# Two layers' weight tiles moved to other byte offsets within their SBUF partitions

## The chip, the core and the metric

The kernel runs on one core of a Trainium2 chip. The metric is the device time of one execution in microseconds (us). The median of three runs of the kernel before is 1143.83 us (1143.75 to 1143.92). The trace shown here is of one further execution, which took 1143.75 us; between its first and its last instruction lie 1142.0 us, called its span.

## The reference, cut to what matters

x has the shape (2, 4096, 192), all in float32. A causal convolution with seven taps per head comes first, then two feed-forward layers on 8192 tokens, each with its own w_in (192 x 2048) and w_out (2048 x 192):

```python
w = softmax(weight)                      # (8 heads, 7 taps)
x = conv(x, w)                           # per head of 24 channels, causal
h = x @ w_in1;  g = h * clip(h + 3, 0, 6) / 6;      x = g @ w_out1
h = x @ w_in2;  g = where(h > 0, h, exp(min(h, 0)) - 1);  out = g @ w_out2
```

## The kernel before, in words

Everything is kept transposed: channels on the partitions, tokens along the free dimension. The 8192 tokens are worked in 16 blocks of 512 tokens, 256 of either batch. A layer's 2048 hidden units are cut in 16 slices of 128, so a "slot" is one layer, one block, one slice; there are 2 x 16 x 16 = 512 slots, in an order written out by hand in `slots`.

To keep float32 accuracy with the type fp32r, each operand is split in a high and a low part. For a slot, `mm1` (L490 in the trace) issues five matmuls into a PSUM bank `h`: the high weights `wi{l}h` with the token operands opA and opB, the low weights `wi{l}l` with opA, and `wi{l}r` (the channels past 128, high in one half of the partitions and low in the other) with opC and opD. VectorE and ScalarE turn `h` into `g` and split it into `gh` and `gl`. Four slots later `mm2` (L533) issues five matmuls per slot with the second weights `wo{l}`: three with gh, two with gl.

From the 36th slot on each matmul is cut into a lower half (partitions 0 to 63) and an upper half (64 to 127), which the array runs side by side; two generators, `lower` and `upper`, hand them to TensorE's queue in turn, one of each. Each matmul instruction brings its own weight load (LDWEIGHTS, shown as engine PEld): 64 or 128 rows by 128 columns of four bytes, which is 512 bytes of each partition, or by 66 columns. The next weights are loaded while the current matmul streams its 512 tokens.

The weights stay in SBUF for the whole kernel, in the pool `const`, which has one buffer for each name. In a partition wi0h, wi0l, wi0r, wi1h, wi1l and wi1r take 8192 bytes each, wo0 and wo1 24,576 each. They are written only once: `load_w` brings raw 64-bit numbers in by DMA, `decode` makes float32 of them, and `split_w` writes the parts by a ScalarE copy and one or two VectorE subtractions. This goes on beside the matmuls until about 292 us; in the first 31 us the matmuls wait for it and for the convolution.

Places in SBUF: the program puts 16 KiB of descriptors and a few constants ahead of the pools, so that `const` begins at byte 16,512 of each partition, which is 32 x 512 + 128. The unused tile `gap0` (96 words, 384 bytes) moves wi0h to byte 16,896 = 33 x 512. All weight tiles are multiples of 512 bytes long, so each of them, and each of their 128-column pieces, begins at a multiple of 512. The tokens' operands (opA to opD, gh, gl) begin at multiples of 512 as well. Not all tiles do: `heads`, a stationary operand of the first matmuls, begins 160 bytes past one, and the convolution reads `xT0` and `xT1` from 320, 384, 448 and 480 bytes past one, and from one to six words further on for the later taps.

The lines that the change touches are these; the rest of the kernel refers to the tiles through `wi[l]` and `wo[l]` only:

```python
const.tile([P, 96], F32, name="gap0")
cv.tile([P, 80], F32, name="gap1")
wi = [{n: const.tile([P, FF], F32R, name=f"wi{l}{n}") for n in ("h", "l", "r")} for l in range(2)]
wo = [const.tile([P, NF, 2 * D], F32R, name=f"wo{l}") for l in range(2)]
```

Of the kernel before, what the change touches and what calls it, by code (L numbers as in the profile page):

```python
# [8 lines left out]
F32 = mybir.dt.float32  # L9
F32R = mybir.dt.float32r  # L10
# [7 lines left out]
P = 128  # L18
# [37 lines left out]
def conv_moe_moe2(ctx: ExitStack, tc: tile.TileContext, x, weight, w_in1, w_out1, w_in2, w_out2, out):  # L56
# [18 lines left out]
    B, S, D = x.shape  # L75
    H, K = weight.shape
    FF = w_in1.shape[1]
    NT = B * S
    NF = FF // P
# [10 lines left out]
    const = ctx.enter_context(tc.tile_pool(name="const", bufs=1))  # L90
# [10 lines left out]

    w_in = (w_in1, w_in2)
    w_out = (w_out1, w_out2)
    const.tile([P, 96], F32, name="gap0")
    cv.tile([P, 80], F32, name="gap1")
    wi = [{n: const.tile([P, FF], F32R, name=f"wi{l}{n}") for n in ("h", "l", "r")} for l in range(2)]
    wo = [const.tile([P, NF, 2 * D], F32R, name=f"wo{l}") for l in range(2)]

    ident = few.tile([P, P], F32, name="ident")
    relay = few.tile([1, 1], F32, name="relay")  # L110
# [192 lines left out]
    def conv_r(b):  # L303
        a = yield from taps_vector(b, 1)
        lh, hl = opnd[0, b][2:]
        T0, T1 = slice(0, HB), slice(HB, NB)
        act.copy(hl[LO, T0], a[LO])
        act.copy(lh[UP, T1], a[UP])
        yield
        act.copy(lh[UP, T0], a[LO])  # L310
        act.copy(hl[LO, T1], a[UP])
        yield
        vec.tensor_tensor(out=lh[LO, T0], in0=a[LO], in1=hl[LO, T0].bitcast(F32), op=ALU.subtract)
        vec.tensor_tensor(out=hl[UP, T1], in0=a[UP], in1=lh[UP, T1].bitcast(F32), op=ALU.subtract)
        yield
        act.copy(hl[UP, T0], lh[LO, T0].bitcast(F32))
        act.copy(lh[LO, T1], hl[UP, T1].bitcast(F32))
        yield
# [366 lines left out]
    with tc.manual_schedule():  # L685
# [13 lines left out]
        r = conv_r(0)  # L699
# [97 lines left out]
    with tc.manual_schedule():  # L797
        ends = {}
        n = {LO: 0, UP: BEHIND}
# [47 lines left out]
```

## Time and profile before

| | |
|---|---|
| median of three runs | 1143.83 us (1143.75 to 1143.92) |
| profiled execution | 1143.75 us |
| its span | 1142.0 us |
| PE (matmul) busy | 1132.0 us, 99%, 9507 instructions |
| PEld (weight load) busy | 1020.9 us, 89%, 9507 instructions |
| DVE (VectorE) busy | 918.7 us, 80% |
| ACT (ScalarE) busy | 929.7 us, 81% |
| granted TensorE clock, mean | 0.999 |

Busy means that at least one instruction of the engine was in flight. Matmuls are pipelined: one takes 386 ns from its start to its end, but the next of the same half starts long before that end, so the pace is read from starts. The weight loads overlap the matmuls.

### The profile page before, as it was taken

The page shows a single profiled execution, that of the slowest core. Times are in us where ns is not written, and L with a number is a line of the kernel's source. Part 1 is how long each engine was busy: PE and PEld are TensorE (multiplying, and loading weights), DVE is VectorE, ACT ScalarE, POOL GpSimd, SP SyncE. Part 2 cuts the span into 40 slices and gives each one's busy share as a digit, 9 for nine tenths or more (in the row PEclk, how much of TensorE's full clock was granted, in tenths as well). Part 3 has the DMA queues.
Part 4 walks back from the last instruction along what each step waited for, and adds up shares of the span by engine and source line. Part 5 has one row for each costly group of instructions (what it writes and reads, how often), then busy time and mean ns, then how long its engine had stood idle before and what let it go on. Part 6 is the DMA issues. An engine that isn't in the chain of part 4 may idle for free.

```text
span 1142.0 us, 25136 instructions
## 1 busy us (share of the span) xinstructions
PE 1132.0 (99%) x9507; PEld 1020.9 (89%) x9507; DVE 918.7 (80%) x1560; ACT 929.7 (81%) x1685; POOL 44.7 (4%) x490
## 2 busy tenths in 40 slices
PE   8999999999999999999999999999999999999998
PEld 6788998988888999999999999999988889888887
DVE  7997999988887968778687887968767666677765
ACT  6876777788888787887878878787886888898986
POOL 0000000000000000000000000000000000000000
PEclk9999999999999999999999999999999999999999
DMA  6422012010010100101001010100000000000001
GB/s 184 112 66 44 22 43 47 29 29 1 2 29 1 27 3 4 26 2 28 2 13 18 1 29 1 24 7 1 15 2 15 2 10 6 15 15 15 13 6 26
DMA packets 105370, 26.80 MB, mean 23 GB/s; under 512 B 96416, under 2 KB 104096, under 8 KB 105248
## 3 DMA queue, kind: packets, MB, share of 16 engines
q1 hardware_dynamic: 104960, 24.99, 10.3%
q8 instruction: 74, 1.21, 0.5%
q14 instruction: 48, 0.39, 0.1%
q10 hardware_dynamic: 288, 0.20, 0.1%
HBM read 18.87 MB, written 6.29 MB: 22 GB/s over the span
## 4 chain that ended last, share of the span: by engine, by line
PE 96%; DVE 2%; ACT 1%; issue 0%; ACTq 0%; DVEq 0%
PE p L533 50%; PE h L490 46%; ACT u L50 1%; DVE acc L50 0%; DVE xw L50 0%; ACT opC L50 0%; DVE g L50 0%; DVE gl L50 0%; ACT opD L50 0%; DVE wi0r L50 0%; DVE cw L50 0%; DVE diag L50 0%; ACT L50 0%; DVE wo L50 0%; ACT gh L50 0%
## 5 line engine op out<-in xcount | busy, mean ns | idle before, releaser
L533 PE MATMUL p<-gh,wo 64*128 64x512 f32 (+1 forms) x2978 | 598.5, 386 | 0.0
L50 DVE SCALAR_TENSOR_TENSOR g<-u,h 128x512 f32<-128x512 f32 x512 | 350.0, 684 | 190.3 <-ACT u L50 185.3
L533 PE MATMUL p<-gl,wo 64*128 64x512 f32 (+2 forms) x1985 | 481.5, 386 | 0.0
L533 PEld LDWEIGHTS p<-gh,wo 64*128 64x128 f32 (+1 forms) x2978 | 433.6, 184 | 28.9 <-ACT gh L50 0.2
L50 DVE TENSOR_TENSOR gl<-g,gh 128x512 fp32r<-128x512 f32 x512 | 350.2, 684 | 2.9 <-ACT gh L50 2.4
L50 ACT CAST gh<-g 128x512 fp32r<-128x512 f32 x512 | 311.3, 608 | 13.4 <-DVE g L50 13.1
L533 PEld LDWEIGHTS p<-gl,wo 64*128 64x128 f32 (+1 forms) x1985 | 292.0, 160 | 20.6 <-DVE gl L50 0.4
L50 ACT ACTIVATE u<-h,three 128x512 f32<-128x512 f32 x256 | 176.1, 688 | 103.6 <-PE h L490 101.1
L50 ACT ACTIVATE u<-h 128x512 f32<-128x512 f32 x256 | 152.6, 596 | 55.3 <-PE h L490 54.4
L490 PE MATMUL h<-opA,wi1h 64*128 64x512 f32 x512 | 182.6, 388 | 0.2
L490 PE MATMUL h<-opA,wi1l 64*128 64x512 f32 x512 | 182.2, 388 | 0.0
L490 PE MATMUL h<-opB,wi1h 64*128 64x512 f32 x512 | 181.5, 386 | 0.0
L490 PE MATMUL h<-opA,wi0h 64*128 64x512 f32 (+1 forms) x476 | 170.8, 389 | 0.5 <-ACT opA L50 0.3
L490 PE MATMUL h<-opB,wi0h 64*128 64x512 f32 (+1 forms) x476 | 170.4, 387 | 0.0
L490 PE MATMUL h<-opA,wi0l 64*128 64x512 f32 (+1 forms) x476 | 170.3, 387 | 0.0
L50 ACT ACTIVATE u<-u 128x512 f32<-128x512 f32 x256 | 161.9, 632 | 8.3
L490 PE MATMUL h<-opC,wi1r 64*128 64x512 f32 x384 | 140.5, 386 | 0.0
L490 PE MATMUL h<-opD,wi1r 64*128 64x512 f32 x384 | 140.4, 386 | 0.0
L490 PE MATMUL h<-opC,wi0r 64*128 64x512 f32 (+1 forms) x366 | 135.1, 387 | 0.6 <-ACT opC L50 0.6
L490 PE MATMUL h<-opD,wi0r 64*128 64x512 f32 (+1 forms) x366 | 134.9, 387 | 0.0
L50 DVE SCALAR_TENSOR_TENSOR acc<-xT,taps,acc 128x256 f32<-128x256 f32 (+1 forms) x180 | 105.6, 603 | 0.1
L490 PEld LDWEIGHTS h<-opA,wi1h 64*128 64x128 f32 x512 | 94.2, 184 | 7.9 <-DVE g L50 2.7
(89 smaller groups left out, 1213.3 us busy)
## 6 DMA issues: line engine op xcount, KB each, us to landing
raw<-in_moe_w_out_dram SPq DMA_DIRECT2D x16, 384.0 KB, 3.2
out_dram<-z SPq DMA_DIRECT2D x180, 32.0 KB, 1.6
raw<-in_moe_w_in_dram SPq DMA_DIRECT2D x7, 512.0 KB, 4.0
x_sq<-in_x_dram SPq DMA_DIRECT2D x112, 32.0 KB, 2.2
raw<-in_moe_w_in_dram SPq DMA_DIRECT2D x8, 256.0 KB, 3.9
xr_sq<-in_x_dram SPq DMA_DIRECT2D x56, 32.0 KB, 2.2
x_sb<-in_x_dram SPq DMA_DIRECT2D x4, 128.0 KB, 3.6
raw<-in_moe_w_in_dram SPq DMA_DIRECT2D x4, 128.0 KB, 3.5
```

The source lines that it names most:

```text
L50: return fn(*args, **kw)
L490: mm = nc.tensor.matmul(h, k, m[half], start=low and i == 0, stop=high and i == len(todo) - 1)
L533: nc.tensor.matmul(p[:n, cols], k[:, :n], m[half, cols], start=first and not end and k is not w0l, stop=last and end == 1 and cols.stop == NB)
```

## The change

The 384 bytes of `gap0` are dealt out in three parts: 128 bytes ahead of layer 1's weights, 192 between the layers, 64 behind. The order of the tiles becomes wi0h, wi0l, wi0r, wo0, wi1h, wi1l, wi1r, wo1. Layer 1's weights now begin at 16,640 = 32 x 512 + 256, layer 2's at 16,640 + 49,152 + 192 = 65,984 = 128 x 512 + 448. The pool ends at byte 115,200 as before, so that every other tile stays at its place. No instruction is added, removed or put in another order.

```diff
     w_in = (w_in1, w_in2)
     w_out = (w_out1, w_out2)
-    const.tile([P, 96], F32, name="gap0")
     cv.tile([P, 80], F32, name="gap1")
-    wi = [{n: const.tile([P, FF], F32R, name=f"wi{l}{n}") for n in ("h", "l", "r")} for l in range(2)]
-    wo = [const.tile([P, NF, 2 * D], F32R, name=f"wo{l}") for l in range(2)]
+    wi, wo = [], []
+    for l, ahead in enumerate((32, 48)):
+        const.tile([P, ahead], F32, name=f"gap{l + 2}")
+        wi.append({n: const.tile([P, FF], F32R, name=f"wi{l}{n}") for n in ("h", "l", "r")})
+        wo.append(const.tile([P, NF, 2 * D], F32R, name=f"wo{l}"))
+    const.tile([P, 16], F32, name="gap4")
```

## Rows read from the trace of the kernel before

**Rows 1.** The page's chain of work that ended last: by engine, by line.
```profile
PE 96%; DVE 2%; ACT 1%; issue 0%; ACTq 0%; DVEq 0%
PE p L533 50%; PE h L490 46%; ACT u L50 1%; DVE acc L50 0%; DVE xw L50 0%; ACT opC L50 0%; DVE g L50 0%; DVE gl L50 0%; ACT opD L50 0%; DVE wi0r L50 0%; DVE cw L50 0%; DVE diag L50 0%; ACT L50 0%; DVE wo L50 0%; ACT gh L50 0%
```

**Rows 2.** That chain in order of time, 500 to 520 us: start, duration (us), work.
```profile
503.86 0.91 PE p L533 x8
```

**Rows 3.** PE by form: rows*columns of weights, count | busy us, mean ns | idle.
```profile
L533 PE MATMUL p<-gh,wo 64*128 64x512 f32 x2878 | 570.7, 386 | 0.0
L533 PE MATMUL p<-gl,wo 64*128 64x512 f32 x1019 | 346.3, 386 | 0.0
L533 PE MATMUL p<-gl,wo 64*66 64x512 f32 x900 | 319.4, 386 | 0.0
L490 PE MATMUL h<-opA,wi1h 64*128 64x512 f32 x512 | 182.6, 388 | 0.2
...
L490 PE MATMUL h<-opA,wi0h 64*128 64x512 f32 x440 | 156.9, 388 | 0.0
...
L490 PE MATMUL h<-opC,wi1r 64*128 64x512 f32 x384 | 140.5, 386 | 0.0
...
L490 PE MATMUL h<-opC,wi0r 64*128 64x512 f32 x330 | 121.0, 386 | 0.0
...
L533 PE MATMUL p<-gh,wo 128*128 128x512 f32 x96 | 27.0, 389 | 0.0
...
L490 PE MATMUL h<-opA,wi0h 128*128 128x512 f32 x36 | 13.9, 396 | 0.5 <-ACT opA L50 0.3 <-DVE g L50 0.2
```

**Rows 4.** PEld, the weight loads, by form.
```profile
L533 PEld LDWEIGHTS p<-gh,wo 64*128 64x128 f32 x2882 | 415.6, 184 | 25.1 <-ACT gh L50 0.2 <-ACT y L50 0.2
...
L533 PEld LDWEIGHTS p<-gl,wo 64*66 64x66 f32 x900 | 119.5, 133 | 7.4
...
L533 PEld LDWEIGHTS p<-gh,wo 128*128 128x128 f32 x96 | 18.0, 188 | 3.8
```

**Rows 5.** Timeline, 704.3 to 705.2 us: start, duration (us), engine, line, work.
```profile
704.48 0.43 PE L533 MATMUL p<-gl,wo 64*66 64x512 f32 x2
704.57 0.18 PEld L490 LDWEIGHTS h<-opA,wi1h 64*128 64x128 f32 x1
...
704.71 0.39 PE L490 MATMUL h<-opA,wi1h 64*128 64x512 f32 x1
704.71 0.18 PEld L490 LDWEIGHTS h<-opB,wi1h 64*128 64x128 f32 x1
...
704.94 0.39 PE L490 MATMUL h<-opB,wi1h 64*128 64x512 f32 x1
```

**Rows 6.** Timeline, 566.5 to 567.2 us.
```profile
566.64 0.46 PE L533 MATMUL p<-gl,wo 64*66 64x512 f32 x2
566.75 0.18 PEld L490 LDWEIGHTS h<-opA,wi1h 64*128 64x128 f32 x1
...
566.87 0.39 PE L490 MATMUL h<-opA,wi1h 64*128 64x512 f32 x1
```

**Rows 7.** The convolution's second stretch of matmuls, timeline of PE.
```profile
17.40 6.21 PE L290 MATMUL psc<-xT,diag 128*128 128x256 f32 x28
```

**Rows 8.** Loads of the tile heads: duration min/median/max (ns), first and last start (us).
```profile
L211 PEld LDWEIGHTS pt<-etap,heads x4: 283/328/328, 3.9 to 4.5; 8*128 8x128 f32 x4
```

**Rows 9.** Loads of the tile diag, in the same view.
```profile
L290 PEld LDWEIGHTS psc<-xT,diag x56: 187/189/337, 6.6 to 23.0; 128*128 128x128 f32 x56
```

**Rows 10.** DVE by form: the gate, the taps, and two forms that write weights.
```profile
L50 DVE SCALAR_TENSOR_TENSOR g<-u,h 128x512 f32<-128x512 f32 x512 | 350.0, 684 | 190.3 <-ACT u L50 185.3
L50 DVE SCALAR_TENSOR_TENSOR acc<-xT,taps,acc 128x512 f32<-128x512 f32 x84 | 62.6, 746 | 0.0
...
L50 DVE TENSOR_TENSOR wo<-xw,wo 128x256 fp32r<-128x256 f32 x16 | 6.7, 418 | 0.0
...
L50 DVE TENSOR_TENSOR wi1l<-xw,wi1h 128x512 fp32r<-128x512 f32 x4 | 2.7, 684 | 0.0
```

**Rows 11.** The chain in order of time, 0 to 40 us.
```profile
10.77 0.43 DVE wi0r L50
...
16.82 0.63 DVE wo L50 x2
```

## Prediction

> **What bounds the kernel now.** I read the page's chain of waits first, then that chain in order of time, then the groups by form of PE and of PEld, then the timeline around single matmuls.
>
> The chain belongs to TensorE for 96% of the span, half of it in the second matmuls and nearly half in the first [rows 1]. So only three things can move the time: the pace of the matmuls, the few waits between them, and the first 31 us, in which the chain runs through VectorE and ScalarE.
>
> The pace is read from the chain in order of time: eight matmuls take 0.91 us [rows 2]. Lower and upper halves alternate, so these are four of each, and one half starts a matmul every 0.91 / 4 = 0.2275 us; I use 227 ns. The counts by form are 2878 + 1019 + 900 second matmuls of 64 rows, and of the first ones three forms of 512, three of 440, two of 384 and two of 330: 4797 + 4284 = 9081, or 4541 pairs [rows 3]. Of the uncut kind with 128 rows there are 96 gh, two gl for each three gh, that is 64, and five forms of 36: 340 [rows 3]. Then (4541 + 340) x 227 ns = 1108 us of a span of 1142.0. What is left, 34 us, is the beginning, the tail and a few waits. One nanosecond on the pace of both kinds is worth 4.9 us, 0.43% of the time.
>
> **The change, part by part.** No instruction comes or goes. What changes is the address from which 9081 + 340 weight loads read, and to which some 90 instructions of the preparation write.
>
> *The loads.* In the steady stretch a load starts at the same instant as its half's current matmul, 704.71, lasts 0.18 and has ended at 704.89; the matmul that needs it starts at 704.94 [rows 5]. The mean load of 64 rows and 128 columns takes 184 ns [rows 4], so 227 - 184 = 43 ns are spare; of these some 3 pass between the two starts, and I count 40. A load of 128 rows takes 188 [rows 4] and has 4 fewer. Up to 40 ns more on each load cost nothing here, since the streaming of the current matmul covers them. Without that cover each further nanosecond is 4.9 us.
>
> What does a row cost that doesn't begin at a multiple of 512? The trace has one such stationary operand: `heads`, 160 bytes past, loads in 328 ns, the slowest of four [rows 8]. The like loads of `diag`, at multiples of 512, take up to 337 ns, and these longest ones are the earliest, under the same slow matmuls of the first 9 us [rows 9]. So a shifted load is 9 ns shorter than an aligned one, not longer; eight rows against 128 may account for some of that, as 64 rows against 128 make 4 ns in the later loads. From below I bound the shift by -9 ns, from above by the fixed part of a load paid a second time. That part follows from two widths: (184 - 133) / (128 - 66) = 0.82 ns a column [rows 4], 105 ns for 128 columns, and so 184 - 105 = 79 ns fixed. I take 0, which is nearest to `heads`; a gain on a load that is hidden is worth nothing either.
>
> *The loads against the streaming.* Could the new address change what the reads of the weights do to the reads of the tokens? Before, both begin at a multiple of 512, and the load mostly starts with the matmul, so they might meet at each step in the same way. If that cost time, a load that starts later would meet the tokens elsewhere and change the pace. In two places a load waited: at 704.57, 0.09 us after its half's matmul at 704.48, and at 566.75, 0.11 us after the one at 566.64. The next matmul of that half starts at 704.71 and 566.87, both 0.23 us after the one before, as ever [rows 5, 6]. A width of 66 columns instead of 128 doesn't show either: the eight matmuls in 0.91 us hold both widths [rows 2, 4]. So I take 0 for this too. The bounds: below, the pace of the convolution's matmuls. They are of another type and 256 columns, each with a full load as well, and 28 of them take 6.21 us [rows 7]; less the 0.4 us of the last one that is 5.8 / 27 = 215 ns. So 12 ns per matmul could be the price of a collision, if all the difference were one. Above, I have no row; the same 12 ns serve.
>
> The Trainium skill, page "TensorE: Matmul & The Clock Gate", section "LDWEIGHTS (loading the stationary operand)", puts a load at columns / 1.2 in ns, independent of the rows: 107 ns for 128 columns, an estimate by that page. The trace agrees in the slope, 0.82 against 0.83 ns a column, though not in the whole, 184 ns. By that rule two halves whose loads stream one after the other need 213 of 227 ns, and then 7 ns more on each would already set the pace.
>
> By the rows alone the like reckoning is 2 x 105 = 210 of 227 ns, thus 8 ns spare per load in place of 40, if the two halves' loads share one path. This lowers the point at which the slower rival decides, and is why I give that rival more than a token chance.
>
> *The writes of the preparation.* ScalarE and VectorE write the weights once; their targets now begin at another multiple of 64 bytes. A tap reads xT at odd places and takes 746 ns where the gate of the same size takes 684 [rows 10]. That is at most 62 ns for a shifted operand, and it has an operand more from `taps`, so most of it may be that. Below, a write that gains nothing: 0. On the chain only those of the first 31 us count, such as 0.43 us for a wi0r or 0.63 us for two of wo [rows 11]; about ten of them make 10 x 62 ns = 0.6 us at most. Later ones lie beside matmuls on engines that are busy for 80%. I take 0.
>
> *The other order of the tiles.* wi1 and wo0 change places by whole multiples of 8 KiB. In the trace wi and wo, which lie up to 98 KB apart, stream at the same 386 to 388 ns [rows 3], so the far place costs nothing.
>
> **The sum** is 0 + 0 + 0 on 1143.75 us of the profiled execution (1142.0 of span and 1.75 around it), 0.08 us from the median 1143.83. I predict 1143.8 us. A measurement of this kernel tells about 0.2%, 2.3 us, from no change.
>
> **The rivals.**
>
> *Loads outlast their matmul (slower).* A row of 512 bytes that begins at 256 or 448 spreads over two stretches of 512. If the load starts anew for the second one, it pays the fixed part again: 184 + 79 = 263 ns plus the 3, against 227, 39 ns on 4541 pairs, and 188 + 79 + 3 - 227 = 43 ns on 340: 177 + 15 = 192 us, 1336 us. It decides from 40 ns on, or from 8 ns if both halves' loads share a path; just beyond that point it costs 4.9 us a nanosecond. For it: the loads are spread over 89% of the span. Against it: `heads` [rows 8, 9]. Chance 0.13, half of it for the far end. Smaller losses, through the preparation or through loads that come late after a wait, 0.06: 1146.5 to 1150 us.
>
> *The shift frees the streaming (faster).* If weights and tokens do collide while aligned, the pace could fall from 227 towards 215: 4881 x 12 ns = 59 us, 1085 us at the far end, and 1132 us if a fifth of that is freed. For it: each of these matmuls has the same 12 ns more than the convolution's [rows 2, 7]. Against it: late loads and narrow loads keep the pace [rows 5, 6]. Chance 0.14, half of it for more than 12 us. Shorter waits by another timing of the halves, 0.07: up to 5 us of the 34 outside the pace, 1139 us.
>
> *The tiles don't lie where they should.* Then nothing happens, and the time is the forecast's. The sums of the tile sizes give 16,640 and 65,984 bytes, so I give this no share of its own.
>
> **How the numbers follow.** No change has 0.60, faster 0.14 + 0.07 = 0.21, slower 0.13 + 0.06 = 0.19. The likeliest gives 1143.8 us. The range goes 2.5 ns of pace, 12 us, to each side: 1132 to 1156. Outside remain the far halves of both large rivals, 0.07 + 0.065, so that it should hold about 86%, and a narrower one would cut into their near halves. Within the likeliest case alone I would say 1141.5 to 1146.1.
>
> **What would show it.** If I am right, the load of the 64 x 128 form stays near 184 ns, eight matmuls of the chain keep 0.91 us, and the PE groups keep 386 ns. A load above 190 ns with the pace unchanged would show the first step wrong but its cover right. A load above 224 ns, or eight matmuls in more than 0.92 us, would prove the slower rival. Eight in 0.87 us or less with unchanged loads would prove that aligned reads collide, and my argument from the late loads wrong. A difference between the stretches of layer 1 (up to 250 us mostly) and layer 2 would show that the offset within 512 bytes, 256 or 448, has a price of its own. A longer first 31 us at the same pace would point to the writes.

## The result and the profile after

The changed kernel takes 1152.42 us (median of four runs, 1151.95 to 1152.64), against 1143.88 us for the kernel before in the same runs (1143.75 to 1143.92). The ratio is 1.0074, with a 95% interval of 1.0062 to 1.0086. The time lies in the range given, but not at the forecast: I had called no change the likeliest, and the kernel is slower by 8.5 us.

The chain of waits still belongs to TensorE, as in [rows 1]:

```profile
PE 97%; DVE 1%; ACT 1%; issue 0%; DMA 0%; ACTq 0%; DVEq 0%
```

No wait on another engine has grown in it, so I looked for a change of pace. The matmuls by form, as in [rows 3], show in which layer (after x the count: busy us and mean ns of one):

```profile
L536 PE MATMUL p<-gh,wo 64*128 64x512 f32 x2878 | 586.5, 388 | 0.0
...
L493 PE MATMUL h<-opA,wi1h 64*128 64x512 f32 x512 | 189.4, 392 | 0.0
...
L493 PE MATMUL h<-opA,wi0h 64*128 64x512 f32 x440 | 156.9, 389 | 0.0
...
L493 PE MATMUL h<-opC,wi1r 64*128 64x512 f32 x384 | 144.1, 389 | 0.0
...
L493 PE MATMUL h<-opC,wi0r 64*128 64x512 f32 x330 | 120.9, 387 | 0.0
```

Layer 1's matmuls (wi0) take what they took, within 1 ns. Layer 2's (wi1), in the two forms shown, went from 388 to 392 and from 386 to 389 ns; the second weights, in which both layers stand together, from 386 to 388. The loads themselves, as in [rows 4], have not grown:

```profile
L536 PEld LDWEIGHTS p<-gh,wo 64*128 64x128 f32 x2882 | 425.9, 184 | 28.7 <-ACT y L50 0.2
...
L536 PEld LDWEIGHTS p<-gl,wo 64*66 64x66 f32 x900 | 119.7, 133 | 9.0
```

The chain in order of time, as in [rows 2] (start, duration in us, work), first in a stretch of layer 1, then in one of layer 2:

```profile
455.99 0.91 PE p L536 x8
...
457.13 0.91 PE h L493 x8
```

```profile
970.41 0.70 PE h L493 x6
...
971.58 0.70 PE p L536 x6
```

Eight in 0.91 us are 227 ns a pair, as before. Six in 0.70 us are 0.70 / 3 = 233 ns. To put one number on it I took the distance from each 64-row matmul's start to the start of the next but one, which is the same half's next, left out the waits (over 300 ns), and averaged over the stretches in which for some 90 matmuls to either side only layer 1's or only layer 2's first weights are in use:

| | layer 1 alone, ns | layer 2 alone, ns |
|---|---|---|
| before | 227.1 | 226.9 |
| after | 227.1 | 230.3 |

Layer 2 has 256 slots of 9.5 pairs; 2432 x 3.4 ns = 8.3 us of the 8.5. The beginning is nearly as before: matmuls run steadily from 31.17 us on, against 30.93. So layer 2, with its weights at 448, runs slower, and layer 1, with its weights at 256, does not; whether the offset, the layer or the order of the tiles does it is left to the experiments.

### The profile page after: what moved, and what is told of

Its sections match the earlier page's. It is cut to its first block, busy times and chain, and to the rows that moved or that the text cites. A ratio compares the mean times of both kernels' runs of the same rounds, so it can differ in the third digit from the quotient of the medians.

```text
span 1150.9 us, 25136 instructions
## 1 busy us (share of the span) xinstructions
PE 1140.7 (99%) x9507; PEld 1022.4 (89%) x9507; DVE 918.2 (80%) x1560; ACT 930.7 (81%) x1685; POOL 44.6 (4%) x490
## 4 chain that ended last, share of the span: by engine, by line
PE 97%; DVE 1%; ACT 1%; issue 0%; DMA 0%; ACTq 0%; DVEq 0%
PE p L536 51%; PE h L493 46%; DVE acc L50 0%; DVE xw L50 0%; ACT u L50 0%; DVE wi0r L50 0%; ACT opC L50 0%; DMA traw<-in_weight_dram 0%; ACT xw L50 0%; DVE cw L50 0%; DVE diag L50 0%; DVE wo L50 0%; ACT gh L50 0%; ACT opD L50 0%; PE pso L438 0%
## 5 line engine op out<-in xcount | busy, mean ns | idle before, releaser
L536 PE MATMUL p<-gh,wo 64*128 64x512 f32 (+1 forms) x2978 | 614.2, 388 | 0.0
L536 PE MATMUL p<-gl,wo 64*128 64x512 f32 (+3 forms) x1985 | 496.1, 388 | 0.0
L536 PEld LDWEIGHTS p<-gh,wo 64*128 64x128 f32 (+1 forms) x2978 | 443.9, 184 | 32.5 <-ACT y L50 0.2
L536 PEld LDWEIGHTS p<-gl,wo 64*128 64x128 f32 (+2 forms) x1985 | 296.4, 160 | 24.1 <-DVE gl L50 0.4
L493 PE MATMUL h<-opA,wi1h 64*128 64x512 f32 x512 | 189.4, 392 | 0.0
L493 PE MATMUL h<-opB,wi1h 64*128 64x512 f32 x512 | 188.8, 392 | 0.0
L493 PE MATMUL h<-opA,wi1l 64*128 64x512 f32 x512 | 187.8, 389 | 0.0
L493 PE MATMUL h<-opD,wi1r 64*128 64x512 f32 x384 | 144.4, 390 | 0.0
L493 PE MATMUL h<-opC,wi1r 64*128 64x512 f32 x384 | 144.1, 389 | 0.0
L493 PEld LDWEIGHTS h<-opB,wi1h 64*128 64x128 f32 x512 | 94.3, 184 | 6.0
```

What stands on the lines that cost most here:

```text
L493: mm = nc.tensor.matmul(h, k, m[half], start=low and i == 0, stop=high and i == len(todo) - 1)
L536: nc.tensor.matmul(p[:n, cols], k[:, :n], m[half, cols], start=first and not end and k is not w0l, stop=last and end == 1 and cols.stop == NB)
```

## Experiments

All were run once each, beside a run of the kernel before on the same chip (1144.2 to 1144.6 us). The edits are against the changed kernel's loop over `(32, 48)`; a word is four bytes. "Tokens" are the streaming operands opA to opD, gh and gl. The pace is the number explained above. A gap given as 0 is left out.

| kernel | weights (layer 1 / 2), bytes past a multiple of 512 | tokens | pace, layer 1 / 2, ns | us |
|---|---|---|---|---|
| before | 0 / 0 | 0 | 227.1 / 226.9 | 1143.88 |
| changed | 256 / 448 | 0 | 227.1 / 230.3 | 1152.42 |
| e1_256_256 | 256 / 256 | 0 | 227.2 / 226.9 | 1143.85 |
| e2_448_448 | 448 / 448 | 0 | 231.9 / 231.5 | 1168.24 |
| e3_448_256 | 448 / 256 | 0 | 230.6 / 226.9 | 1152.95 |
| e4_0_0 | 0 / 0, new order | 0 | 227.0 / 226.9 | 1144.56 |
| e5_448_tok448 | 448 / 448 | 448 | 227.1 / 226.8 | 1143.93 |
| e6_0_tok64 | 0 / 0 | 64 | 231.5 / 231.2 | 1165.36 |
| e9_tmp448 | 0 / 0 | 0 | 227.1 / 226.9 | 1143.83 |
| e7_wi448 | wi 448, wo 0 | 0 | 230.0 / 229.9 | 1157.61 |
| e8_wo448 | wi 0, wo 448 | 0 | 229.6 / 229.5 | 1155.87 |
| e10_wo_gp448 | wi 0, wo 448 | op 0, gh and gl 448 | 229.7 / 229.7 | 1156.99 |
| w128 | 128 / 128 | 0 | 232.5 / 232.6 | 1169.47 |
| w192 | 192 / 192 | 0 | 231.0 / 231.6 | 1166.45 |
| w224 | 224 / 224 | 0 | 233.2 / 233.3 | 1172.84 |
| w288 | 288 / 288 | 0 | 232.7 / 232.8 | 1170.39 |
| w320 | 320 / 320 | 0 | 233.1 / 233.1 | 1171.79 |

### Offset, layer or order

e1_256_256:

```diff
-    for l, ahead in enumerate((32, 48)):
+    for l, ahead in enumerate((32, 0)):
...
-    const.tile([P, 16], F32, name="gap4")
+    const.tile([P, 64], F32, name="gap4")
```

> Both layers' weights begin 256 bytes past a multiple of 512. Theory A (the price hangs on the offset, and 448 has it while 256 has none): 1143.8 us, within 1 us, and a pace of 226 to 227 ns in both layers' stretches. Theory B (layer 2's stretches have no reserve, so that any start off a multiple of 512 slows them): 1152 us, like the changed kernel. Theory C (the new order of the tiles costs): 1152 us as well.

e2_448_448:

```diff
-    for l, ahead in enumerate((32, 48)):
+    for l, ahead in enumerate((80, 0)):
```

> Both layers' weights begin 448 bytes past a multiple of 512. Theory A: layer 1's stretches slow down as well, by the same 3.5 ns a pair on some 2400 pairs, so 1152.4 + 8.5 = 1161 us, within 2 us. Theory B: layer 1 keeps 226 to 227 ns, 1152 us. Theory C: 1152 us.

e3_448_256:

```diff
-    for l, ahead in enumerate((32, 48)):
+    for l, ahead in ((1, 32), (0, 48)):
...
-        wi.append({n: const.tile([P, FF], F32R, name=f"wi{l}{n}") for n in ("h", "l", "r")})
-        wo.append(const.tile([P, NF, 2 * D], F32R, name=f"wo{l}"))
+        wi[l] = {n: const.tile([P, FF], F32R, name=f"wi{l}{n}") for n in ("h", "l", "r")}
+        wo[l] = const.tile([P, NF, 2 * D], F32R, name=f"wo{l}")
```

> The offsets are exchanged: layer 1's weights 448 past a multiple of 512, layer 2's 256 past one, with layer 2's tiles ahead of layer 1's. Theory A: about 1152 us, within 2 us, but now it is the stretches of layer 1 that run at 229 to 233 ns, those of layer 2 at 226 to 227. Theory B: layer 2 stays slow, 1152 us. Theory C (order alone): no forecast for which stretch.

e4_0_0:

```diff
-    for l, ahead in enumerate((32, 48)):
+    for l, ahead in enumerate((96, 0)):
...
-    const.tile([P, 16], F32, name="gap4")
```

> The new order of the tiles (wi0, wo0, wi1, wo1) with both layers at multiples of 512, as before. Theories A and B: 1143.8 us, within 1 us. Theory C: 1152 us.

Both at 256: 1143.85 us. Exchanged: 1152.95 us. Order alone: 1144.56 us. So theory A holds, B and C fall. In the exchanged kernel's forms the slow layer has changed sides:

```profile
L493 PE MATMUL h<-opA,wi1h 64*128 64x512 f32 x512 | 190.2, 389 | 0.2
...
L493 PE MATMUL h<-opA,wi0h 64*128 64x512 f32 x440 | 166.2, 392 | 0.0
```

Only the sum was off: with 448 in both layers the time is 1168.24 us where I expected 1161. In the like stretch of layer 1, between 35 and 95 us, before layer 2 begins, the two kernels with layer 1 at 448 don't keep the same pace. The windows of before, of e2_448_448 and of e3_448_256 (length, PE busy and the number of matmuls, then the other engines, the granted clock 1.00, DMA):

```profile
35.00:95.00 60.00, 60.00 (x267) 48.38 (x266) 59.08 (x112) 47.84 (x88) 0.00 (x0) 1.00 0.31 81
```

```profile
35.00:95.00 60.00, 60.00 (x260) 47.34 (x259) 58.05 (x110) 47.04 (x86) 0.00 (x0) 1.00 0.31 81
```

```profile
35.00:95.00 60.00, 60.00 (x263) 47.83 (x262) 58.69 (x112) 47.61 (x88) 0.00 (x0) 1.00 0.31 81
```

260 and 263 matmuls of the same form in 60 us, where layer 1's weights stand at the same offset in both. From start to start the matmuls of e3_448_256 go round in about 226, 229 and 232 ns there, and e6_0_tok64 and w192 keep the same round; in e2_448_448 most distances are 232 to 234 ns. So an uneven offset allows at least two rhythms; what chooses between them the runs leave open.

### Against the tokens, or by itself

e5_448_tok448, where all that lies behind the weights moves down by 64 bytes:

```diff
-    for l, ahead in enumerate((32, 48)):
+    for l, ahead in enumerate((80, 0)):
...
-    const.tile([P, 16], F32, name="gap4")
```

> All weights 448 past a multiple of 512 as in the run with 448 twice (1168.2 us), and now the tokens' operands too: all tiles behind the weights move down by 64 bytes, so that opA to opD, gh and gl begin 448 past. Theory R (what counts is where the weights begin against the tokens): both begin alike again, 1144 us and a pace of 227 ns. Theory S (what counts is where a weight row begins by itself): 1168 us, within 3 us. Theory T (every operand off some multiple costs by itself): over 1168 us.

e6_0_tok64:

```diff
-    cv.tile([P, 80], F32, name="gap1")
+    cv.tile([P, 96], F32, name="gap1")
...
-    for l, ahead in enumerate((32, 48)):
+    for l, ahead in enumerate((96, 0)):
...
-    const.tile([P, 16], F32, name="gap4")
```

> Weights at multiples of 512 as before, everything from the convolution's tiles on 64 bytes up, so that opA to opD, gh and gl begin 64 past: the weights stand to the tokens as in the run with 448 twice. Theory R: about 1168 us, within 3 us. Theory S: 1144 us. Theory T: over 1144 us, by an amount of its own.

e9_tmp448, which leaves the tokens where they were and moves only what VectorE and ScalarE work in, and the convolution's xT, which TensorE reads in the first 24 us alone:

```diff
-    cv.tile([P, 80], F32, name="gap1")
+    cv.tile([P, 64], F32, name="gap1")
...
-    for l, ahead in enumerate((32, 48)):
+    for l, ahead in enumerate((96, 0)):
...
-    const.tile([P, 16], F32, name="gap4")
...
+    gp.tile([P, 16], F32, name="gap5", bufs=1)
```

> Weights and the tokens' operands (gh, gl, opA to opD) at multiples of 512 as before; only the tiles that VectorE and ScalarE work in (acc, g, u, xw, cw, s1), which TensorE does not read, are moved to 448 past one. Theory R in the form that the two reads of TensorE alone decide: 1144 us, within 1 us, and 227 ns. If what counts is TensorE's reads against those of the other engines: over 1155 us.

This is the clearest pair of the study. With weights and tokens both at 448 the price is gone: 1143.93 us. With the weights back at multiples of 512 and the tokens 64 past, it is there: 1165.36 us. The first row is of e5, the second of e6:

```profile
L493 PE MATMUL h<-opA,wi1h 64*128 64x512 f32 x512 | 183.9, 388 | 0.2
```

```profile
L493 PE MATMUL h<-opA,wi1h 64*128 64x512 f32 x512 | 179.1, 393 | 0.0
```

The mean of one is what to read here, 388 against 393 ns. e9_tmp448 takes 1143.83 us, so the places of the tiles that it moves don't matter, at the one offset tried. (The sums y0 and yr, which e6 moves together with the tokens, were not moved by themselves.) What matters is how TensorE's two operands, weights and tokens, stand to each other.

### Which distances are even

w128, w192, w288, w320 and w224 have one offset for both layers, as w128 here:

```diff
-    for l, ahead in enumerate((32, 48)):
+    for l, ahead in enumerate((0, 0)):
...
-    const.tile([P, 16], F32, name="gap4")
+    const.tile([P, 96], F32, name="gap4")
```

> Both layers' weights 128 past a multiple of 512, tokens at multiples of 512. If the price comes from a start off a multiple of 128 (a row of 512 bytes then touches five stretches of 128 in place of four): 1144 us. If it comes from a start off a multiple of 256: some 1168 us. If it grows with the distance to the next multiple of 512: between 1144 and 1168.

> Both layers' weights 192 past a multiple of 512. Off a multiple of 128 (by 64, as 448 is) and off a multiple of 256: some 1168 us by either rule, within 3 us. If only the last 64 bytes ahead of a multiple of 512 are bad: 1144 us.

> Both layers' weights 288 past a multiple of 512, which is 32 past the good offset 256, tokens at multiples of 512. If the places count in steps of 64 bytes or more: 1144 us. If in steps of 32 or less: 1160 to 1170 us, like the other shifts; under 1140 us would mean that the even offset is not the best.

> Both layers' weights 320 past a multiple of 512, 64 past the next lower multiple of 256, tokens at multiples of 512. If only multiples of 256 are even: 1164 to 1171 us, like 128, 192 and 448. If a lag in one direction is free (weights behind the tokens): 1144 us.

> Both layers' weights 224 past a multiple of 512, 32 short of a multiple of 256. If only multiples of 256 are even: 1164 to 1171 us. If the even place is broader on this side than on the other, where 32 past cost as much as any: 1144 us. Below 1140 us would show a better place than the even one.

All five cost 22.6 to 29.0 us over 1143.88. So 128 bytes apart is as bad as 64, 32 as bad as 128, on either side; of all distances tried, counted within 512 bytes, only 0 and 256 are even. None is better than the even one: no version here beats the kernel before, and the best only equal it (both layers at 256, weights and tokens at 448, the kernel with the other engines' tiles moved). Distances of less than 32 bytes were not tried.

### Which loads pay

e7_wi448 lays the four wi groups and then wo, e8_wo448 the reverse, with the first kind at 448 and the second at 0; e7:

```diff
-    for l, ahead in enumerate((32, 48)):
-        const.tile([P, ahead], F32, name=f"gap{l + 2}")
+    const.tile([P, 80], F32, name="gap2")
+    for l in range(2):
         wi.append({n: const.tile([P, FF], F32R, name=f"wi{l}{n}") for n in ("h", "l", "r")})
+    const.tile([P, 16], F32, name="gap4")
+    for l in range(2):
         wo.append(const.tile([P, NF, 2 * D], F32R, name=f"wo{l}"))
-    const.tile([P, 16], F32, name="gap4")
```

> Both layers' first weights (wi) 448 past a multiple of 512, both layers' second weights (wo) at multiples. If each load pays for itself: 9 of 19 half matmuls of a slot load wi, so 1144 + 24 x 9/19 = 1155 us. If a few shifted loads already undo an even pace of all: near 1168 us.

> The reverse: both layers' second weights (wo) 448 past a multiple of 512, the first at multiples. If each load pays for itself: 1144 + 24 x 10/19 = 1157 us. If a few shifted loads undo the even pace of all: near 1168 us.

e10_wo_gp448 is e8_wo448 with gh and gl at 448 too, and with them y0, yr and the tiles that e9_tmp448 moves:

```diff
-    cv.tile([P, 80], F32, name="gap1")
+    cv.tile([P, 64], F32, name="gap1")
...
+    op.tile([P, 16], F32, name="gap5", bufs=1)
```

> wo, gh and gl begin 448 past a multiple of 512, wi and opA to opD at multiples: each load stands evenly to the tokens of its own matmul, but the first wi load of a slot runs while gl streams, and the first wo load while opC or opD streams. If a load is priced against the tokens that stream while it runs: 2 of 9.5 pairs are uneven, 24 x 2/9.5 = 5 us, about 1149 us. If it is priced against the tokens of its own matmul: 1144 us, within 1 us.

1157.61 and 1155.87 us are near the sums by count, 1155 and 1157, so at first each load seems to pay for itself. e10 shows that it isn't that simple. It should have given 1149 us if a load is priced against the tokens that stream meanwhile, 1144 if against its own; it took 1156.99 us, as much as the two others, though far fewer loads are uneven by either reckoning. What the three share is that the places change twice in each slot and half. The forms of e10 show the price where both readings see nothing uneven: wi1l and opA lie at multiples of 512, and so does wi1r, which is loaded while opA streams through wi1l, and yet this is the slowest form.

```profile
L495 PE MATMUL h<-opA,wi1l 64*128 64x512 f32 x512 | 189.7, 394 | 0.0
L495 PE MATMUL h<-opA,wi1h 64*128 64x512 f32 x512 | 187.7, 388 | 0.0
```

The stretch ahead of the two halves says the same: from 70 to 75 us the three longest distances of each slot, 233 to 236 ns, come after the third matmul with gh, after opA with wi0l and after opC with wi0r, where the tokens that stream and the weights that load stand alike. So a disturbance seems to be paid for some matmuls after it. With which tokens exactly a load has to be even stays open.

## Why the prediction was wrong

**The bound** was right. TensorE's pace sets the time, one nanosecond on all pairs is worth some 4.9 us, and 3.4 ns on half of them are the result. That this lies in the range was luck: the change put one layer at 256, which costs nothing. With both at 448 the time is 1168.24 us, well outside.

**The loads' own duration**, step one, was right: 184 ns stayed 184, and the longest load of 64 rows in the changed kernel took 188, less than the 227 ns of a pair. The slower rival, which I had built on that, did not happen. Its second sign misled: eight matmuls in more than 0.92 us were to prove it, and at the 233 ns of the stretch of layer 2 shown above eight take 0.93 us, with loads as short as before. The sign of the two layers' stretches came true, though 448 has no price of its own: it has one only against tokens that stand elsewhere.

**The loads against the streaming** is the step that failed. I took 0, and gave the rival of a collision one sign only: that the aligned state collides and the shift frees it. The reverse is true; being aligned is the even state, and e5 and e6 show both halves of it. I had written "Above, I have no row; the same 12 ns serve" and then not made a rival of that bound. It measured 3.4 ns for layer 2 and up to 6.4 ns (w224).

My argument for 0 was that late loads meet the tokens elsewhere and keep the pace, and I showed two that did [rows 5, 6]. I stopped reading one step too early. In both places the late load ends after its own matmul has started (704.57 + 0.18 against 704.71, 566.75 + 0.18 against 566.87), so that this start can't tell what the load did. That half's next two distances are 235 and 229 ns in the one place, 232 and 236 in the other: the pace did break.

Two places were also too small a choice. In the trace of before up to 1134 us there are 38 loads of 64 rows which started 10 to 215 ns after their half's matmul and whose own matmul still followed that one within 240 ns: 21 have 226 or 227 ns, 17 have 229 to 240. In some of the 17 the load ended too late for the matmul that was due, and that alone may have held it; not so in this one, in the timeline of before:

```profile
293.03 0.39 PE L533 MATMUL p<-gl,wo 64*66 64x512 f32 x1
293.06 0.18 PEld L490 LDWEIGHTS h<-opA,wi1h 64*128 64x128 f32 x1
...
293.27 0.39 PE L490 MATMUL h<-opA,wi1h 64*128 64x512 f32 x1
```

The load starts 0.03 us late and has ended 0.02 us before the next matmul, which comes after 0.24 us, not 0.23. After such late loads and after waits the pace of before stays uneven for some microseconds and then settles, which its chain in order of time shows too, first soon after a wait, then later:

```profile
296.89 0.93 PE p L533 x8
...
301.45 0.91 PE p L533 x8
```

Both were to be seen before the change: an uneven pace of 229 to 236 ns existed, and a reader who had asked when it appears would have had the row for the upper bound. That these uneven stretches have the same cause as the shifted kernels' is only argued, from their like size.

**The writes and the order of the tiles** were right at 0: the steady matmuls begin 0.24 us later, but so does the very first matmul (4.16 against 3.90 us), ahead of any write of a weight; and e4_0_0 takes 1144.56 us against 1144.63 for the kernel before in that job.

The Trainium skill says that PE and ACT never wait on anyone (page "SBUF — State Buffer", section "Who interferes with whom"). For the other engines e9_tmp448 agrees, 1143.83 us, as far as its one move of their tiles can tell. It also says that loading the next weights doesn't steal read bandwidth from the running matmul (page "TensorE: Matmul & The Clock Gate", section "Step-by-step: what each phase is for"). Whether it is bandwidth that is lost here no run shows, but the two reads are not free of each other in time: the same instructions take 1143.9 or 1172.8 us by the distance of the two operands alone, and the measurement decides.

## What to carry to other kernels

Where matmuls with their own weight loads set the pace, look at where the two operands of TensorE begin in a partition, against each other: here a multiple of 256 bytes apart was even, and 32, 64 or 128 bytes off cost about 2% to 2.5% in every placement tried for all weights. A bound for which no row exists belongs among the rivals with both signs. And an argument from chosen rows needs the count of the rows that say otherwise.

## What the runs showed of the hardware that was not expected

- The distance between weights and tokens within 256 bytes is worth up to 29 us of 1144, at a granted clock of 0.999 to 1.000 and with mean loads of 184 to 185 ns for 64 rows and 128 columns in all runs.
- It is the distance and not the place: weights and tokens both at 448 are as good as both at 0 (1143.93 and 1143.88 us).
- The same offset can give two paces: 263 or 260 matmuls in the same 60 us, with layer 1's weights at 448 in both.
- A change of place within a slot costs like many uneven loads: 1156.99 us in e10_wo_gp448, by a mechanism that stays open.
